# One fixed instruction order exchanged for another, found with a new account of when loads land, in an attention and gated feed-forward kernel

## The chip, the core and the metric

The kernel runs on one core of a Trainium2 chip. The metric is device time in microseconds (us) of the one launch. Five engines work side by side, each through its own instructions in the order in which they stand: TensorE (PE in the profile, with its weight loads as PEld), VectorE (DVE), ScalarE (ACT), GpSimd (POOL) and SyncE (SP), which issues every DMA of this kernel.

## What is computed

For each of 4 batches and 8 heads (768 tokens, 64 features a head) an attention over a local window and block summaries, then a gated feed-forward layer over the joined heads:

```python
k_sum = k.reshape(B, H, nb, block, D).max(axis=3)      # 24 blocks of 32 tokens
v_sum = v.reshape(B, H, nb, block, D).mean(axis=3)
mask_l = np.abs(pos[:, None] - pos[None, :]) < 16
scores = concat([where(mask_l, scale * q @ k.T, -1e9), scale * q @ k_sum.T + log(32)])
a = softmax(scores);  x = a @ concat([v, v_sum])       # (4, 768, 512)
...
xk = mu_k * x + (1 - mu_k) * x_prev;  xr = mu_r * x + (1 - mu_r) * x_prev
out = sigmoid(xr @ w_r) * (maximum(xk @ w_k, 0) ** 2 @ w_v)
```

`x_prev` is `x` one token earlier. The weights come in 64-bit floats and are unpacked on the chip.

## The kernel before

**Tiling.** Heads are taken in pairs, so a batch has four sets (`load_set`), each with the pair's keys `kt`, and its values in two halves `vx`. A set serves two units (`unit`), one for each half of the 768 tokens, each with its own query load `qt`. Unit (b, p, h) below is batch b, pair p, half h. A unit is: scores on PE (L476), mask and running minimum on DVE (L486), six exponentials on ACT (L490), the normalization on DVE, ACT or POOL (L501, L507, L512), two groups of three transposes on PE (L524), their copies (L530 on ACT, L532 on DVE), and the product with the values on PE (L539). The block maxima of the keys are taken on DVE (L412, L416, L420) and copied into `kt` on DVE or POOL (L424). In batch 0 the block means of the values come from PE (L436, then L444, with copies on ACT in L443 and L446 between and behind) and are spread into `vx` on POOL (L450). The product of a unit needs that spread.

**Feed-forward.** Mixing with the token before is L572 to L585; the gate is three products a chunk on PE (L626 to L628) and a sigmoid (L640); the first expert product is L655, its square and the split into a high and a low part L661 to L670, the second expert product L680 and L706, and the result goes out from L716. Batch b's feed-forward is interleaved with the attention of batch b+1.

**Weights.** Twenty loads of 512 KB (`weight`, L320) go through three staging tiles `st`. Each is scaled on ACT (L327), shifted and joined on DVE (L331, L335), rounded to the high part on ACT, POOL or DVE (L344, L346, L348), and the low part is a subtraction on DVE (L349).

**Order.** Nothing is scheduled at run time: the table `ORDER` lists 1910 numbered operations. A number may have a letter that sends the operation to another engine (D, A or P for DVE, ACT or POOL), and every engine gets its operations in the order in which they stand in the table. `Plan.schedule` walks the table once and gives each operation a start time from durations in `LENGTH`, hand-over times in `LATENCY` and a line of DMA figures. Those times decide three things of the program: how many filler products on a zero tile stand ahead of each real PE operation in the opening (L753, only where the plan sees PE idle), which buffer of a pool an operation gets, and which DVE operation some POOL operations have to wait for (the loop under `TIE`). All else that the DMA figures did, they did in the search that wrote the table, which is not in the file.

Of the kernel before, what the change touches and what calls it, by code (L numbers as in the profile page):

```python
# [20 lines left out]
P = 128  # L21
# [34 lines left out]
DMA_FIRST, DMA_ISSUE, DMA_START, DMA_EACH, DMA_END, DMA_BYTES_PER_NS = 740, 470, 900, 100, 1200, 400.0  # L56
FIXED_MORE = 320000
# [11 lines left out]
181 187 179 185 205 209 213 207 211 190D 1 3 4 24 191 5 193 212 43 25 6D 196 197 206 61 50 49 7 26 27 203 276 44 192D  # L69
28 45 17 92 204 214 18 210 19 194 20 52 51 80 69 208 21 215 195 216 53 46 71 217D 198 218 70 199 274 54P 219 200A 227  # L70
47 72 220 395 221 73P 234 68 300 235 372P 22 36 238 232 230 228 236 222D 252 233 231 373 396 37 237 239 229 38 253 255
39 254 62 240D 224 40 263 259 241 257 261 223 397 55 249 243D 374D 63 242D 375 64 262 264 258 256 244 225A 56 277 260
245D 376P 399 57 286 246 265D 377 58 619 324 104 585 388 65 93 81 247D 282 278 280 288 266 284 59 60 248 378D 267D 400
82 398 83 379 66 94 269 289 281 279 287 268 74 250A 301 75 270 380 98 348 643 283 285 381 290D 76 271 389 77 78 675
272 84 403 401 308 291 310 302 306 382D 292D 312 309 383 304 105 95 402 404 273 294 325 275A 313 384 390 293 295 385
86 407D 386D 589 387 99 311 307 303 296 297 405 391 408 106 85 409D 107 87 305 108 298 128 586 406 410 314D 88 411 100
89 109 394 96 393 332 315 423 101 317P 328 116 110 412 129 330 334 326 336 413 102 130 316D 97 349 90 414A 318 91 117
416 415 392 319 299A 424 118 131 119 320 421 132P 354 652 759 761 140 594 134 701 588 417D 331 41 321 422 120D 355 337
322 352 590 121 418 335 103 430 111 141 329 419 358 420 112 360 333 327 323A 425 428 142 133 113 135 338 478P 587 122
431D 647 429 474P 350 356 437 339 114 357 479 340D 341D 115 359 426A 432 427 342 361 351 353 143 433A 434 136 435 152  # L80
343 123 436 144 591 362 137 344 363 595 164 345 364 346 145 606 124 598 125 365D 438 366 439 444 599 367D 347A 153
440A 482 602 604 600 126P 644 146 596 79 368 620 369 445 480 127 154 475 370 165 155 442 371A 156 481 483 157 158 677
443 486 441 484D 476 138 607 487 147 488 451 139 605 627 477 485 489 449 452 601 446 453 603 166 167 148 490 705 149
623 150D 631 159 496 597 447A 151 608D 160 450 456 609 161 491 1145 170 577 492 646 625 629 611P 617 454A 504P 500D
501 621 448 497 578 505 614 457 168 162 163 171 493 494 579 615 172 610 648 649P 580 653 495 169 173 763 506 581 735
702 575 612 654 507 656 658 664 791 508P 502 503 455 509 498 630 499 458 510 632 459 626 463 460 461A 624 613 174D 511
464 538 175 576 665 539 659 622 462 582 471 583 465 468 512 628 584 657 704 706 660 633D 634 472 469 517 592 762 466
# [12 lines left out]
1093P 855 1056 1097 1095 926 927 1057D 1058 1121 836 838 574 1211 867 833 1036 1076 1179 930 1108 1109 856 1593 1077D  # L100
1104 1100 1105 857 858 859 1592 834 1098 1078 1106 1079 1080D 1102 1059D 860 861D 1099 1122 862 1107 868D 1060 863 931
1103 869 1081 895 932 1061 1463 1154 1094 865 1125 1062A 1101 864 1082D 1110D 1111 1127 870 1083 866 928 872 896 1594
897 898 920 921 873 874 1112D 1126 1595 922 1128 1133 871 879 875 1129 1464 1123 923 933 880 888 1131 876 877 940 1469
1124 1132 1084D 899 924 941 889D 1130 1119 1155 1085 1212 1114 1177 1113 881 1115 929 878 944 882D 1134 1135 1116 886
1158 1156 925 1166 1167 883 1468 948D 949 934 884 1086A 1159 1157 1160 1204 1117 935 1203 1210 571 887 893 885 945 890
1648 894 891A 936 892 1162 1207 1136 1137 900 937 1164 1206 1208 1209P 1479P 938 1180 1165 942 939 943 1118 1507 1138D
952D 1470 1139 1120A 1146 901 902 1187 1191 953 954D 950D 946D 1235 951 1140D 1265D 947 907 903 904 905A 1188 1163
1141 908 906 1161 955 1287D 1288 1189 912 915 956 1289D 916 1183 1181 1261 1182 1266 1185 957 1142 1262 1267D 1268
1263D 961 958 959A 1192 962 963 1190 913 1213 1184 1466 1143 1540 917 1471 975 1152 1472 1144 960 1168 1169 1531 1264
1475 1170D 1172 909 976 1186 966 964 965 1193 1171D 1173D 1218 1194 1216 910 1290 967 973 1174 1222 1223 977 978A  # L110
1175D 1214 1224 1220 968 969 1225 1195D 1238 970 1176 1647 1482 1654 971 1196D 1534 1481 911 1197 1217 1247 1248 1215
# [50 lines left out]
class Plan:  # L162
# [697 lines left out]
```

## Time and profile before

| | |
|---|---|
| median of 3 runs | 445.56 us (445.32 to 445.6) |
| the profiled execution | 445.36 us |
| its span, first to last instruction | 443.6 us |
| PE busy | 436.4 us, 98% of the span |
| DVE busy, ACT busy | 297.1 us (67%), 273.3 us (62%) |
| POOL busy | 30.9 us (7%) |
| bytes moved by DMA | 51.95 MB |

The profiled execution is 1.76 us longer than its span and 0.2 us under the median of the runs. Busy time of PE counts the fillers too, which compute nothing. The rows on which the argument rests stand in a section of their own below.

### The profile page before, as it was taken

The numbers are of one execution on the slowest core, as the hardware profiler recorded it, in microseconds if no ns is written. First come the engines' busy times: TensorE is split into PE (matmuls) and PEld (weight loads), VectorE is DVE, ScalarE is ACT, GpSimd is POOL, SyncE is SP. The second block draws the span as 40 slices with busy tenths as digits, with TensorE's granted clock in tenths as the row PEclk, the third lists the DMA queues.
The fourth block names the chain that finished last, engine by engine and source line by source line (L and its number), as shares of the span: only waits on it lengthen the run. The fifth ranks groups of instructions, "written<-read, shape, count | busy, mean of one in ns | idle before, by whom it ended". The sixth has DMA issues, their size and how long they took to land.

```text
span 443.6 us, 9603 instructions
## 1 busy us (share of the span) xinstructions
PE 436.4 (98%) x3582; PEld 375.6 (85%) x3582; DVE 297.1 (67%) x972; ACT 273.3 (62%) x807; POOL 30.9 (7%) x78
## 2 busy tenths in 40 slices
PE   7999999999999999999999999999999999999996
PEld 7877888889888888878898888888888888989885
DVE  3999989998998946648767755557643646444211
ACT  2999999885777597575466666564964315223321
POOL 0140211101030000000000210000000000000000
PEclk9999999999999999999999999999999999999999
DMA  8985868437656170141440143101200010002002
GB/s 309 401 299 194 281 249 265 149 126 227 228 141 253 55 239 27 53 153 55 134 144 19 44 117 105 51 1 42 79 1 1 2 47 1 0 1 95 0 1 95
DMA packets 26878, 51.95 MB, mean 117 GB/s; under 512 B 2512, under 2 KB 14416, under 8 KB 26832
## 3 DMA queue, kind: packets, MB, share of 16 engines
q1 hardware_dynamic: 26832, 51.35, 34.7%
q8 instruction: 28, 0.46, 0.5%
q14 instruction: 18, 0.15, 0.1%
HBM read 43.28 MB, written 6.29 MB: 112 GB/s over the span
## 4 chain that ended last, share of the span: by engine, by line
PE 87%; ACT 5%; DVE 3%; DMA 2%; issue 1%; SPq 0%; DVEq 0%; ACTq 0%
PE mm L655 28%; PE mm L680 25%; PE av L539 5%; PE pt L524 5%; PE sc L476 5%; PE mm L628 4%; PE mm L626 4%; PE mm L627 4%; PE mm L706 4%; PE av L753 2%; ACT y L490 2%; DMA st<-in_w_k 1%; DMA kt<-in_k 1%; DVE y L486 1%; ACT wc L327 1%
## 5 line engine op out<-in xcount | busy, mean ns | idle before, releaser
L655 PE MATMUL mm<-xs,wk_h 128*128 128x384 f32 x512 | 102.0, 341 | 0.6 <-DVE r L663 0.4
L655 PEld LDWEIGHTS mm<-xs,wk_h 128*128 128x128 f32 x512 | 89.5, 188 | 5.7 <-DVE r L663 1.1
L490 ACT ACTIVATE y<-y,mn 128x120 f32<-128x120 f32 x192 | 74.0, 387 | 31.0 <-DVE mn L486 30.8
L680 PE MATMUL mm<-wv_h,kh 128*128 128x512 f32 x168 | 67.2, 400 | 0.0
L680 PE MATMUL mm<-wv_l,kh 128*128 128x512 f32 x168 | 66.3, 395 | 0.0
L655 PE MATMUL mm<-xs,wk_l 128*128 128x384 f32 x256 | 55.3, 337 | 0.0
L665 ACT ACTIVATE r<-r 128x384 f32<-128x384 f32 x64 | 32.7, 520 | 35.0 <-DVE r L663 34.3
L670 DVE TENSOR_TENSOR kl<-r,kh 128x384 fp32r<-128x384 f32 x64 | 35.4, 559 | 26.7 <-ACT kh L669 18.9
L486 DVE CUSTOM_DVE_ANT_0 y<-sc,fixed_sb 128x120 f32<-128x120 f32 x192 | 47.4, 274 | 5.9 <-PE sc L476 3.7
L680 PE MATMUL mm<-wv_h,kl 128*128 128x512 f32 x168 | 49.7, 404 | 0.0
L661 ACT ACTIVATE r<-mm 128x384 f32<-128x384 f32 x42 | 20.5, 489 | 46.2 <-PE mm L655 41.6
L579 DVE SCALAR_TENSOR_TENSOR xa<-vx,fixed_sb,xa 128x384 f32<-128x384 f32 x64 | 39.1, 613 | 10.6 <-ACT xa L572 9.5
L655 PEld LDWEIGHTS mm<-xs,wk_l 128*128 128x128 f32 x256 | 45.6, 188 | 0.0
L585 DVE TENSOR_TENSOR xs<-xa,xs 128x384 fp32r<-128x384 f32 x64 | 35.1, 554 | 5.7 <-ACT xs L582 5.3
L626 PE MATMUL mm<-wr_h,xs 128*128 128x512 f32 x96 | 38.6, 402 | 0.0
L628 PE MATMUL mm<-wr_h,xs 128*128 128x512 f32 x96 | 38.0, 396 | 0.0
L627 PE MATMUL mm<-wr_l,xs 128*128 128x512 f32 x96 | 37.9, 395 | 0.0
L680 PEld LDWEIGHTS mm<-wv_h,kh 128*128 128x128 f32 x168 | 31.6, 188 | 6.2 <-DVE kh L668 0.3
L680 PEld LDWEIGHTS mm<-wv_l,kh 128*128 128x128 f32 x168 | 31.6, 188 | 6.0
L490 ACT ACTIVATION_READ_ACCUMULATOR y<-y,mn 128x1 f32 x192 | 36.3, 189 | 0.0
L680 PEld LDWEIGHTS mm<-wv_h,kl 128*128 128x128 f32 x168 | 30.2, 188 | 5.4
L524 PE MATMUL pt<-fixed_sb,y 128*120 128x128 f32 x192 | 33.2, 282 | 0.0
(76 smaller groups left out, 654.2 us busy)
## 6 DMA issues: line engine op xcount, KB each, us to landing
vx<-in_v SPq DMA_DIRECT2D x32, 384.0 KB
kt<-in_k SPq DMA_DIRECT2D x15, 544.0 KB
qt<-in_q SPq DMA_DIRECT2D x32, 192.0 KB
out<-z SPq DMA_DIRECT2D x23, 256.0 KB
st<-in_vT SPq DMA_DIRECT2D x12, 384.0 KB
st<-in_w_k SPq DMA_DIRECT2D x8, 512.0 KB
st<-in_w_v SPq DMA_DIRECT2D x8, 512.0 KB
st<-in_w_r SPq DMA_DIRECT2D x4, 512.0 KB
```

Source lines behind the costliest of these rows:

```text
L486: op("DVE", "mask", lambda h=h, i=i, var=var: nc.vector.tensor_tensor_reduce(out=y[h].t[:, i, :], in0=sc[h].t[:, i, 0:NK], in1=mask_sb[:, ...
L490: op("ACT", "exp", lambda h=h, i=i: nc.scalar.activation(y[h].t[:, i, :], y[h].t[:, i, :], AF.Exp, bias=mn[h].t[:, i:i + 1], scale=-1.0, a ...
L524: nc.tensor.transpose(out=pt.t[0:NK, i * P:(i + 1) * P], in_=y[h].t[:, i, :], identity=ident_sb)
L579: op("DVE", "mixd", lambda xt=xt, xa=xa, p=p: nc.vector.scalar_tensor_tensor(out=xa.t, in0=xt.t[:, 1 + lo:1 + lo + HT], scalar=mu_sb[:, wh ...
L585: op("DVE", "sub", lambda xa=xa, xh=xh, xl=xl: nc.vector.tensor_tensor(out=xl.t, in0=xa.t, in1=xh.t.bitcast(F32), op=ALU.subtract), reads= ...
L626: nc.tensor.matmul(ps[t].t, xh.t[:, ts], wr_h[:, p, :], start=(p == 0), stop=False)
L627: nc.tensor.matmul(ps[t].t, xh.t[:, ts], wr_l[:, p, :], start=False, stop=False)
L628: nc.tensor.matmul(ps[t].t, xl.t[:, ts], wr_h[:, p, :], start=False, stop=(p == NPAIR - 1))
L655: nc.tensor.matmul(ps.t[:, 0:HT], w[:, j, p, :], x[p][s].t, start=(n == 0), stop=(n == 11))
L665: op("ACT", "square", lambda: nc.scalar.activation(r.t, r.t, AF.Square), reads=[(r, 0)], writes=[(r, 0)])
L670: op("DVE", "sub", lambda: nc.vector.tensor_tensor(out=kl.t, in0=r.t, in1=kh.t.bitcast(F32), op=ALU.subtract), reads=[(r, 0), (kh, 0)], wr ...
L680: nc.tensor.matmul(acc[t].t, a.t[:, t * P:(t + 1) * P], w[:, j, :], start=start, stop=stop)
```

## The change

The change replaces the whole table `ORDER`, and the DMA figures with which its operations are timed. No operation is added or dropped, no duration in `LENGTH` is touched, and no tile changes its size.

```diff
-DMA_FIRST, DMA_ISSUE, DMA_START, DMA_EACH, DMA_END, DMA_BYTES_PER_NS = 740, 470, 900, 100, 1200, 400.0
-FIXED_MORE = 320000
+DMA_FIRST, DMA_ISSUE, DMA_START, DMA_EACH, DMA_END, DMA_BYTES_PER_NS, DMA_COLD = 740, 470, 1000, 50, 650, 400.0, 2240
+FIXED_MORE, KT_MORE = 0, 0
+DMA_STALL = 4200, 500
...
 ORDER = """
-29 8 9 176 0 201 2 23 32 42 12 10 11 48 67 14 13 33 34 15 16 226 35 177 30 31 188 251 178 182 180 189 183 186 184 202
+9 8 176 13 12 199 14 15 16P 29 0 2 201 23 42 10 11 48 32 67 226 177 31 30 1 180 181 184 182 251 33 183 50 49 188 178
...
-        dma, table, kind, shared = 0, None, "M", 0
+        dma, table, kind, shared = DMA_COLD, None, "M", 0
...
-                dma = max(dma, start + DMA_START) + DMA_EACH + o.size / DMA_BYTES_PER_NS
+                begin = max(dma, start + DMA_START)
+                dma = begin + DMA_EACH + o.size / DMA_BYTES_PER_NS
+                dma += DMA_STALL[1] * (begin < DMA_STALL[0] <= dma)
                 o.finish = dma + DMA_END + o.more[1]
...
-               writes=[(kt, f"k{n}")], size=P * (hi - lo) * 4, more=(0, 2 * LATE if b else 0))
+               writes=[(kt, f"k{n}")], size=P * (hi - lo) * 4 + (KT_MORE if (b, p, n) == (0, 0, 1) else 0), more=(0, 2 * LATE if b else 0))
```

Three lines are added above the code, so a line of the changed kernel has a number 3 higher than before. Three places show what the new table does; in all three `kt`, `qt`, `vx`, `st`, `wc`, `av`, `mm`, `sc` and `pt` are the tiles named above, and the number behind a name is its buffer.

SP, the first eight loads of the program, before:

```order
L386 DMA kt0_61<-in_k 128x1088
L386 DMA kt1_62<-in_k 128x528
L386 DMA kt1_62<-in_k 128x560
L465 DMA qt0_65<-in_q 128x384
L288 DMA fixed_sb_151<-in_fixed 128x556
L465 DMA qt1_66<-in_q 128x384
L320 DMA st0_136<-in_w_r 128x1024
L320 DMA st1_137<-in_w_r 128x1024
```

and now:

```order
L389 DMA kt0_61<-in_k 128x560
L389 DMA kt0_61<-in_k 128x528
L468 DMA qt0_65<-in_q 128x384
L389 DMA kt1_62<-in_k 128x1088
L291 DMA fixed_sb_151<-in_fixed 128x556
L323 DMA st0_136<-in_w_r 128x1024
L468 DMA qt1_66<-in_q 128x384
L323 DMA st1_137<-in_w_r 128x1024
```

The keys of pair 0, in two parts, and the first query load moved ahead of the keys of pair 1; the four loads ahead of `fixed_sb` (mask and constants) are the same four.

PE, from the last score of unit (0, 3, 0) over the product of unit (0, 1, 0) (`av` from `vx`), before:

```order
L476 MATMUL sc_143<-kt_64,qt_65 64x120 x2
L444 MATMUL mm_150<-sp_88,fixed_sb 24x128
L753 MATMUL av_146<-still 128x128 x7
L539 MATMUL av_146<-pts_104,vx_70 64x64
L539 MATMUL av_146<-pts_103,vx_70 64x64
...
L436 MATMUL mm_147<-vx_73,fixed_sb 32x128 x2
L436 MATMUL mm_147<-vx_72,fixed_sb 32x128 x2
...
L524 MATMUL pt_145<-fixed_sb,y_90 120x128 x3
```

and now:

```order
L479 MATMUL sc_143<-kt_64,qt_65 64x120 x2
L527 MATMUL pt_145<-fixed_sb,y_92 120x128 x3
L447 MATMUL mm_150<-sp_88,fixed_sb 24x128
L756 MATMUL av_146<-still 128x128
L439 MATMUL mm_147<-vx_74,fixed_sb 32x128 x2
L439 MATMUL mm_147<-vx_73,fixed_sb 32x128 x2
...
L756 MATMUL av_146<-still 128x128 x2
L542 MATMUL av_146<-pts_104,vx_72 64x64
L542 MATMUL av_146<-pts_103,vx_72 64x64
```

The block means of pair 2 (`mm_147`) stood behind the product and stand ahead of it, in the place of most of the fillers; the second group of transposes of unit (0, 1, 0) stood ahead of the scores of unit (0, 3, 0) and stands behind them.

POOL, the stretch that holds all of its weight roundings (L346) before:

```order
L512 TENSOR_SCALAR y_91<-y_91,rc_102 128x120 x3
L346 TENSOR_SCALAR wk_h<-wc_141 128x512
L450 COPY vx_71<-vm_84 24x768
L575 TENSOR_SCALAR xa_111<-vx_68,om_sb 128x384
L575 TENSOR_SCALAR xa_113<-vx_75,om_sb 128x384
L346 TENSOR_SCALAR wv_h<-wc_141 128x512
```

and the same part of its list now:

```order
L349 TENSOR_SCALAR wk_h<-wc_141 128x512
L349 TENSOR_SCALAR wv_h<-wc_141 128x512
L453 COPY vx_71<-vm_84 24x768
L453 COPY vx_73<-vm_85 24x768
L427 COPY kt_62<-ks_80 128x12x24
L349 TENSOR_SCALAR wv_h<-wc_141 128x512
L453 COPY vx_76<-vm_86 24x768
L349 TENSOR_SCALAR wv_h<-wc_142 128x512
L349 TENSOR_SCALAR wv_h<-wc_141 128x512
```

With two of `wr_h` further up, POOL now rounds seven weights where it rounded two; ACT rounds 10 (14 before) and DVE 3 (4 before). Over the whole program ACT has 16 of the additions of epsilon (10 before), 42 of the copies behind transposes (31) and 35 of the relu (42); DVE has the rest of each.

## Rows read from the trace of the kernel before

**Rows 1.** The page: its first line, the busy time of each engine, and the granted clock of PE in tenths, in 40 slices of the span.

```profile
span 443.6 us, 9603 instructions
PE 436.4 (98%) x3582; PEld 375.6 (85%) x3582; DVE 297.1 (67%) x972; ACT 273.3 (62%) x807; POOL 30.9 (7%) x78
...
PEclk9999999999999999999999999999999999999999
```

**Rows 2.** Busy time of each engine by stretch: the stretch and its length, then busy time and count of instructions for PE, PEld, DVE, ACT and POOL, the granted clock, the DMA share and GB/s.

```profile
0.00:10.00 10.00, 7.48 (x66) 7.13 (x67) 4.01 (x20) 2.03 (x5) 0.41 (x5) 1.00 0.82 298
...
40.00:60.00 20.00, 19.89 (x161) 16.90 (x160) 18.85 (x59) 19.13 (x50) 3.13 (x5) 1.00 0.77 263
60.00:80.00 20.00, 19.42 (x180) 16.40 (x178) 19.41 (x57) 19.89 (x61) 2.81 (x4) 1.00 0.66 221
80.00:100.00 20.00, 20.00 (x117) 16.74 (x116) 19.76 (x57) 16.53 (x45) 3.03 (x8) 1.00 0.42 136
```

**Rows 3.** The group of the fillers among the groups of instructions of PE: busy time, mean ns of one, idle time before them.

```profile
L753 PE MATMUL av<-still 128*128 128x128 f32 x112 | 16.0, 300 | 1.0 <-POOL still L747 1.0
```

**Rows 4.** The timeline of the opening: start, length, engine, line, operation, with the idle time of the engine before it and what ended it where there was any.

```profile
4.13 1.42 DVE L412 TENSOR_REDUCE kg<-kt 128x48 f32<-128x768 f32 x2 [4.13 <-DMA kt<-in_k]
6.59 0.17 DVE L416 TENSOR_REDUCE kg<-kt 128x1 f32<-128x16 f32 x1 [1.04 <-DMA kt<-in_k]
6.68 0.54 DVE L412 TENSOR_REDUCE kg<-kt 128x24 f32<-128x384 f32 x1
...
8.01 0.84 PE L476 MATMUL sc<-kt,qt 64*64 64x120 f32 x24 [1.53 <-DVE kt L424]
...
8.92 0.28 DVE L486 CUSTOM_DVE_ANT_0 y<-sc,fixed_sb 128x120 f32<-128x120 f32 x1 [0.75 <-PE sc L476]
...
9.25 0.39 ACT L490 ACTIVATE y<-y,mn 128x120 f32<-128x120 f32 x1 [7.24 <-DVE mn L486]
...
12.99 0.97 ACT L507 ACTIVATE y<-y,rc 128x120 f32<-128x120 f32 x3 [0.17 <-DVE rc L498]
...
17.69 0.94 DVE L412 TENSOR_REDUCE kg<-kt 128x48 f32<-128x768 f32 x1
17.73 0.26 ACT L446 COPY vm<-mm 24x128 f32<-24x128 f32 x1 [0.25 <-PE mm L444]
...
18.54 0.21 ACT L495 ACTIVATE sm<-sm 128x6 f32<-128x6 f32 x1
...
19.19 0.65 POOL L424 COPY kt<-ks 128x288 f32<-128x288 f32 x1
```

**Rows 5.** The timeline of SP's queue: start, length, line, what is loaded, how many in a row.

```profile
7.12 1.06 SPq L386 DMA_DIRECT2D kt<-in_k  x2
...
20.19 1.18 SPq L391 DMA_DIRECT2D vx<-in_v  x2
22.02 7.17 SPq L465 DMA_DIRECT2D qt<-in_q  x3
```

**Rows 6.** One of the sums of SP's waits: the line that waited, what it waited for, us in total, times, longest. The issue of a load waits until the load eight places ahead of it has landed.

```profile
SPq L391 <- DMA st<-in_w_r: 1.9, 2, 0.9
```

**Rows 7.** The timeline at the end of the opening, with the last large group of fillers.

```profile
24.09 1.83 PE L753 MATMUL av<-still 128*128 128x128 f32 x14
...
24.55 0.26 ACT L446 COPY vm<-mm 24x128 f32<-24x128 f32 x1
...
24.95 0.82 POOL L450 COPY vx<-vm 24x768 f32<-24x768 f32 x1 [1.20 <-DVE mn L486]
...
25.84 0.92 PE L539 MATMUL av<-pts,vx 120*64 120x64 f32 x24
...
26.69 0.86 PE L436 MATMUL mm<-vx,fixed_sb 120*32 120x128 f32 x24
```

**Rows 8.** Two of the sums of PEld's waits, at the scores and at the products with the values (line, what ended the wait, us in total, times, longest).

```profile
PEld sc L476 <- issue: 5.3, 19, 0.4
PEld av L539 <- issue: 4.1, 21, 0.4
```

**Rows 9.** The timeline of one load of `w_k` with what waited behind it on ACT, DVE and PE.

```profile
53.25 0.38 SPq L320 DMA_DIRECT2D st<-in_w_k  x1
...
58.77 0.66 ACT L327 ACTIVATE wc<-st 128x512 f32<-128x512 f32 x1 [0.81 <-DMA st<-in_w_k]
...
59.47 0.43 DVE L331 TENSOR_SCALAR wc<-wc 128x512 uint32<-128x512 uint32 x1 [0.83 <-ACT wc L327]
...
61.62 1.66 PE L655 MATMUL mm<-xs,wk_h 128*128 128x384 f32 x8 [0.45 <-DVE r L663]
```

**Rows 10.** The instructions of the line that rounds a weight on POOL: count, shortest, median and longest in ns, first and last start in us.

```profile
L346 POOL TENSOR_SCALAR wk_h<-wc x1: 992/992/992, 53.3 to 53.3; 128x512 fp32r<-128x512 f32 x1
L346 POOL TENSOR_SCALAR wv_h<-wc x1: 837/837/837, 69.5 to 69.5; 128x512 fp32r<-128x512 f32 x1
```

**Rows 11.** The same for one of the forms of the line that rounds a weight on ACT.

```profile
L344 ACT CAST wk_h<-wc x6: 604/619/627, 36.8 to 83.8; 128x512 fp32r<-128x512 f32 x6
```

**Rows 12.** The timeline of DVE around the first of the two on POOL.

```profile
52.50 1.29 DVE L335 SCALAR_TENSOR_TENSOR wc<-st,wc 128x512 uint32<-128x512 uint32 x2
...
53.28 0.99 POOL L346 TENSOR_SCALAR wk_h<-wc 128x512 fp32r<-128x512 f32 x1 [3.86 <-DVE wc L335]
...
53.91 0.95 DVE L412 TENSOR_REDUCE kg<-kt 128x48 f32<-128x768 f32 x1
```

More of the change, by code (lines that the diff above doesn't have):

```diff
@@ L73 @@
[L73 to L87, printed above, removed]
@@ new lines @@
+186 34 35 3 202 4 179 187 189 185 5 205 6P 61 24 203 276 211 209 207 204 212 210 213 190D 191 7 193D 196 208 43 206
+197 214 25 192D 26 17 44 92 27 215D 194 45 18 195 52 216 19 80 28 20 68 218 46 217 51 21 71 53 198 70 54P 227 47 72
+200A 395 219 73P 300 234 238 372P 235 236 69 36 230 237 232 22 224 228 233 220D 252 373 221 396 37 239 229 231 38 222
+259 55 240D 253 374D 39 257 274 40 261 255 260 254 241 263 56 243D 62 223 242D 262 63 264 57 375 244 258 397D 277 58
+64 245 225A 246 398 86 256 388 65P 280 93 399 324 286 284 703 81 265D 59 288 266 268 376P 701 278 247D 282 248 289
@@ new lines @@
+122 430 358 321D 350 331 360 594 425 41 329 337 643 354 103 111 588 60 428 141 420 357 123 338 142 429 426A 132D 590
+112 339 322 431D 591P 361 341 124 133 595 353 113 344 677 323A 437 340D 143 114 760 152 359 345 115 427 351 342 125
+432 355 435 433A 343 362D 606 602 126P 598 438 604 605 603 79 436 363 596 364 600 144D 620 705 153 346 647 127 145 366
+474 478 154 442 365D 367 146 134 155 347A 164 368 156 434 479 444 443 135 157 136 475 597 601 623 137 480 369 607 439
+440A 627 735 158 138P 445D 370 481 476 451 629 371A 482 441 139 486 483 147 487 484 449 477 488 452 625 450 489 485
@@ new lines @@
+1085 1155 1115 1463 1088 882 1206 1116 1166 874 1207 1162 1164 945 1158 1156 875 1086A 880 888 1212 1094 883 876 574
+1589 568 877A 1160 878 1157 1159 889 940 1132 1135D 1167 1208 1136 1138D 886 1204 571 934 884A 941 1161 890 1137 887
+893 885 935 894 891 936 1117 1119 900 937 938 1180 1118 942D 946 947 1466 939 948D 1139 902 1140D 892 1187 1209 953
+954D 1141 901 903 904 907 905A 1183 943 906 1163 908 1181 1120A 949 915 1165 950 1287 909 912 1185 955 951 1189 1592
+956 1190 1186 1265D 916 1288 961 1479 1152 957 1266 958 1191 1464 1182 1474 1188 1210 1142 1593 959 1213 962 963 1184
@@ new lines @@
+1512 1367 1551 1545 1015 1301 1514 1543 1597 1539 1311 1521D 1522 1302A 1390 1524P 1364 1590 1553 1547 1523P 1566
+1312D 1391 1504 1681 1365 1370 1018 1368D 1525 1384 1649 1303 1304 1596 1575 1573 1385 1526D 1278 1527 1282 1325 1305
+1571 1569 1386D 1306 1655 1567 1387 1309 1576 1549 1554 1310 1555 1307 1556 1374D 1308 1316 1577 1506A 1568 1326D 1369
+1570 1317 1327 1578 1328 1318 1313 1375 1314A 1574 1315 1396D 1323 1397 1528 1319 1329 1320 1621 1324 1321 1330 1332
+1599 1333D 1371 1322 1529 1656 1558 1339 1559 1606 1610 1608 1653 1572 1609 1557 1331 1530A 1340 1560 1579 1337 1607
@@ new lines @@
+1600 1604 1580 1605 1334 1602 1581P 1346 1338 1341 1342A 1335 1563 1505 1611 1601 1603 1612D 1336 1582D 1561D 1344
+1398D 1347 1376D 1348 1585 1349 1562 1343 1377 1624 1586 1679 1399 1564 1583 1727 1345 1392D 1393 1351 1613 1635 1728
+1627 1636 1633 1350 1394 1352 1584 1628 1625 1353 1395 1631 1632 1705 1400 1614 1629 1354 1372 1355 1657 1401 1373
+1587 1402 1403A 1616 1626 1615 1617D 1660 1588A 1359 1356 1405 1634 1618 1406D 1357 1407 1630 1358 1637 1619 1666 1382
+1412 1408A 1360 1658 1361 1664 1706 1665 1731 1662 1638 1639 1640D 1667 1668 1409 1659 1682 1661 1404 1620 1643 1380
@@ new lines @@
+1693 1644 1689 1413 1622 1414 1669 1663 1690 1641 1378 1381 1383 1379 1410 1707 1411 1415 1687 1683 1419 1691 1416
+1685 1670D 1729D 1732 1671 1708 1688 1684 1417 1420 1692 1421 1418 1672D 1713 1422A 1424 1730 1673 1735D 1425 1736
+1426 1423 1733D 1734 1714 1431 1427D 1715D 1428 1642D 1429 1433 1430 1432 1645 1434 1435 1674 1675D 1436 1438 1437
+1440 1439 1694 1686 1441D 1646A 1695 1696 1676 1737 1447 1442 1832 1677 1443 1444 1678 1698D 1448D 1701 1716 1449 1445
+1697D 1680A 1446 1702 1450 1739 1452 1740 1738 1451 1741 1453 1833 1709D 1457 1460 1710 1711D 1742 1699 1700D 1712
@@ new lines @@
+1717D 1718 1748 1454 1719D 1720 1455 1703 1749D 1461 1755 1743 1462 1744 1745 1806D 1750 1746A 1807 1828 1751 1721
+1752 1458 1829 1459 1722 1747 1723 1756D 1757 1753 1724 1754 1758 1725 1760 1726 1834 1808 1835 1790 1814D 1809 1759
+1761 1791 1762 1767 1763D 1764 1765A 1769 1768 1836D 1830 1766 1792 1831 1837 1815 1774 1770D 1771 1704 1775 1840D
+1776 1838D 1772 1841 1793 1794 1773 1781 1777 1839 1778 1783 1779A 1782 1784 1788 1785 1780 1818 1789 1786 1842D 1795
+1787 1796 1797 1803 1798 1800 1843 1804 1844 1805 1801 1802 1456 1849 1845D 1810D 1846 1847 1848 1863 1850D 1819 1799
@@ L143 @@
+1811 1820D 1854 1864 1865 1851 1855 1812 1852A 1853 1856 1821 1813 1861 1857D 1858 1859A 1862 1816D 1817 1868 1860
+1869 1870 1866 1867 1871 1872 1873 1875 1874 1876 1877 1882 1878D 1879 1880 1883 1881 1884 1889 1885 1886 1887A 1890
+1891 1896 1892 1893 1894 1822 1888 1895 1897 1823 1901 1898 1824 1899 1826 1825 1902 1903 1900 1904 1827 1907 1905
+1908 1906 1909
 """
```

94 lines of the change are left out of this document (35 added, 59 removed).

## The prediction

> **What bounds the kernel now.** I read the page's first lines, then the busy times by stretch, then the timeline of the opening, then the waits. PE is busy in 436.4 of 443.6 us and its clock is granted in full from the first slice to the last [rows 1], so it is the bound, and neither its products nor its clock are touched by the change. What an order can still take away is time in which PE does nothing that counts. That lies in two places. One is the opening: PE is busy only 7.48 of the first 10 us [rows 2], and 112 filler products of 16.0 us [rows 3] stand where PE would otherwise be empty; most of those 16 us are waiting in disguise. The other is the stretch from 40 to 80 us, where PE lacks 0.11 and 0.58 us, and where ACT is busy 19.89 of 20 us and DVE 19.41 [rows 2]: there the engines that feed PE are full too. From 80 to 100 us PE is full [rows 2]. So the change is worth what it shortens of the opening, plus what it does to the waits of the middle.
>
> **The opening, step by step.** In the opening PE waits for a chain of loads, DVE and ACT. Before, the first score starts at 8.01 us because the third load, a part of pair 0's keys, is first read at 6.59; the masks start at 8.92 and the first exponential at 9.25 [rows 4]. Now the two parts of those keys come first. Together they are 1088 columns, as many as the load of pair 1's keys that came first before and was read at 4.13 [rows 4]; so I take 4.13 for them. Behind that come, on DVE, the maximum of the second part (0.54), the odd columns (0.17), the joining of two maxima (under 0.2) and, now on POOL, the copy (0.65, the longer price [rows 4]), with hand-overs about 0.3: 4.13 + 0.54 + 0.17 + 0.2 + 0.65 + 0.3 = 6.0. The query load, now third, is smaller than the third load of before, so it lands between 4.13 and 6.59. The first score starts between 6.0 and 6.7 instead of 8.01.
>
> Those 1.3 to 2 us are not the gain. The masks also need `fixed_sb`, still fifth with the same four loads ahead, and DVE, which runs its list in order, has the maximum of pair 1's keys (0.94 [rows 4]) ahead of the first mask. Those keys are now the fourth load. SP issues a load when the one eight places ahead of it has landed [rows 6]; its twelfth issue, at 7.12 [rows 5], therefore dates the landing of the fourth load, and the same bytes stand up to there in both lists. 7.12 + 0.94 + about 0.1 for a small operation on `fixed_sb` gives a first mask at 8.2; the first exponential follows 0.33 behind it, as before (8.92 to 9.25 [rows 4]): 8.5. That is 0.7 earlier than before.
>
> From there ACT carries the opening. From 9.25 to 24.81, the end of the copy for the block means of pair 1 [rows 4, 7], it idles only 0.17 + 0.25 between instructions [rows 4]. I counted its list up to that copy in both orders: 18 exponentials, three scalings, three copies behind transposes, two roundings, two normalizations, four copies of block means, one evacuation, one mix in each, and one addition of epsilon (0.21 [rows 4]) that now stands on DVE. So the copy ends at 8.5 + 15.56 - 0.21 = 23.9 if the idle time stays, 23.4 if it goes; I take 23.7. Behind it POOL's spread and the hand-overs took 25.84 - 24.81 = 1.03 [rows 7], which gives the product of unit (0, 1, 0) at 24.7 instead of 25.84: 1.1 earlier. And the block means of pair 2, 26.69 to 27.5 behind that product before [rows 7], now stand ahead of it in the place of fillers, which is another 0.8 us of real work that is already done. The loads allow it. Up to the second value load of pair 1, place 16, the lists hold the same sixteen loads, and the issue at 20.19 [rows 5] dates its landing. The next two value loads moved ahead of one weight load; the issue at 22.02 [rows 5] dates the landing at place 18 before, and one more load behind it lands about 1 us later (the step from 20.19 to 22.02 is two loads): 23. Those means then end at 23.9, ahead of 24.7. **The opening is worth 1.1 + 0.8 = 1.9 us**; if the block means of pair 1 or a DVE step come late by 0.5 it is 1.4, if ACT never idles 2.2.
>
> **Changes of kind on PE.** Each time PE goes over to scores or to a product with values from other work, its weight load stands still for a moment: 5.3 us in 19 places at the scores, 0.28 each, and 4.1 in 21 at the products, 0.20 each [rows 8]. Counted in the two orders, scores are entered from transposes or large products 21 times instead of 26, products with values and block means 19 times instead of 15; the others follow each other directly. That is -5 x 0.28 + 4 x 0.20 = -0.6. Three more times PE goes from transposes to a large product, which has no row of its own; its price lies between 0 and 0.28. So the term lies between -0.6 and 0.2; I take **-0.3**, in the middle of what is left if the new exits cost 0.1 each.
>
> **The middle.** Five more weights are rounded on POOL: 0.84 to 0.99 each there [rows 10] against 0.62 on ACT [rows 11]. What waits is the subtraction on DVE behind it, and with it everything queued on DVE, which is full (19.41 and 19.76 of 20 us [rows 2]). Two of the new five have little DVE work between rounding and subtraction in the list; I charge them 0.3 each on DVE and a third of that on PE: **+0.2**, between 0 (other work on DVE covers it, and ACT is relieved of four roundings) and 1. Loads of weights can still come late. The one case of before is issued at 53.25 and read at 58.77; ACT stood 0.81 for it, DVE 0.83 behind that, and PE 0.45 [rows 9]. The new list still has loads of queries, values and keys ahead of weights in the same stretch, so I leave this loss as it is: 0, between -0.6 (gone) and +1.2 (twice more).
>
> The tail, from the last second product to the last store, has the same operations in the same order, so it costs the same.
>
> **Sum.** 445.36 - 1.9 - 0.3 + 0.2 = 443.4 us for a profiled execution; that of before lies 0.2 us under the median of the runs, so **443.6 us** for the median.
>
> **Rivals.** *The gain is given back.* From 40 to 80 us ACT and DVE are full [rows 2]; a PE that comes 2 us earlier asks for their results 2 us earlier. ACT's chain itself starts only 0.7 us earlier. If ACT and DVE and not PE set the pace there, what remains is those 0.7, and one more late load like that of rows 9 (0.45 to 0.6 on PE) takes the most of it: 445.56 - 0.7 + 0.5 = 445.4, between 444.7 and 446.2. Against it: PE lacks only 0.7 us in those 40 us [rows 2], so PE is still the nearer bound, and four roundings leave ACT.
>
> *POOL holds DVE.* While POOL rounds the weight at 53.28, DVE is still in its second L335, which ends on time (two in 1.29), and the POOL instruction is the long one of the two, 0.99 against 0.84; DVE's L412 behind it takes 0.95 as elsewhere 0.94 [rows 4, 10, 12]. So in that row POOL waited and DVE did not. It need not fall so: if POOL comes first and DVE stands through each of the five, with a DVE that is 97% full the loss goes on to PE: 5 x 0.92 = 4.6 us, 443.6 + 4.6 = 448.2. It ends slower than before from about 2.9 us on, that is from three of the five in full. The Trainium skill has this as a rule (SBUF — State Buffer, "Who interferes with whom"): an instruction of VectorE with two inputs in SBUF and one of GpSimd that reads SBUF exclude each other, and the one that starts first blocks the other for its whole length. By that rule, the trace agrees as far as the row at 53.28 goes, where DVE came first; no row shows the other order.
>
> *More than forecast.* The late load disappears and the two roundings are covered: 443.6 - 0.6 - 0.2 - 0.3 = 442.5, down to 441.9.
>
> *The change does not do what it says*, since the new figures describe the loads no better: then the first score stays near 8 us and the opening gives 0.8 at most, which is within the first rival's time.
>
> **Chances.** A difference of 0.2%, 0.9 us, is about what a measurement of this kernel can tell from no change. The forecast, 442.6 to 444.6, has 0.70; given back, 0.17; POOL holds DVE, 0.06; more than forecast, 0.07. The range of 442.4 to 445.2 holds the forecast, half of the first rival and a little of the last, 0.8 in all. Faster by over 0.2% (under 444.67): 0.70 + 0.07 = 0.77; within 0.2%: 0.17; slower by over 0.2%: 0.06.
>
> **What would show it.** First score at 6.0 to 6.7 us, first exponential at 8.5, the copy of pair 1's block means ending near 23.7, the product of unit (0, 1, 0) near 24.7 with the means of pair 2 ahead of it: each right or wrong by itself. In the middle: PE's busy time from 40 to 80 us no more than 0.7 us short, POOL's roundings 0.84 to 1 us long, L349 and L335 on DVE no longer than before. The forecast is wrong if the first exponential is not earlier than 9.0, or if the product of unit (0, 1, 0) is 1 us earlier and the end is not: then the middle took it, and the waits of ACT for `st` and of DVE for POOL say which way.

## The result: slower by 0.68%

| | before | after |
|---|---|---|
| median of 5 runs (lowest to highest), us | 445.40 (445.11 to 445.60) | 448.29 (447.24 to 449.00) |
| profiled execution, us | 445.36 | 448.97 |
| its span, us | 443.6 | 447.2 |

After to before is 1.0068, with a 95% interval of 1.0057 to 1.0080. The forecast was 443.6 us, and the time lies outside its range. The runs of after also lie further apart, 1.8 us against 0.5.

The page of after: its first line, the busy times and the granted clock, then the shares of the chain that ended last by engine.

```profile
span 447.2 us, 9584 instructions
PE 437.1 (98%) x3570; PEld 374.2 (84%) x3570; DVE 291.6 (65%) x958; ACT 273.7 (61%) x818; POOL 34.6 (8%) x85
...
PEclk9999999999999999999999999999999999999999
...
PE 79%; ACT 11%; DMA 6%; DVE 2%; issue 1%; SPq 0%; DVEq 0%; ACTq 0%
```

The clock is full in both [rows 1]. The same line of the chain before:

```profile
PE 87%; ACT 5%; DVE 3%; DMA 2%; issue 1%; SPq 0%; DVEq 0%; ACTq 0%
```

So ACT and DMA held 7% of it and now hold 17%. The busy times by stretch (columns as in [rows 2]) and the fillers say where:

```profile
0.00:10.00 10.00, 7.90 (x69) 7.58 (x70) 3.48 (x18) 2.15 (x6) 0.86 (x7) 1.00 0.81 286
...
40.00:60.00 20.00, 19.57 (x158) 16.48 (x156) 18.09 (x60) 18.49 (x49) 4.40 (x5) 1.00 0.74 255
60.00:80.00 20.00, 19.01 (x175) 16.21 (x176) 19.13 (x60) 19.12 (x59) 2.48 (x4) 1.00 0.52 174
80.00:100.00 20.00, 17.76 (x100) 13.44 (x99) 16.87 (x45) 15.36 (x35) 1.45 (x4) 1.00 0.64 212
```

```profile
L756 PE MATMUL av<-still 128*128 128x128 f32 x100 | 15.1, 307 | 1.0 <-POOL vx L550 1.0
```

The opening is better: the fillers fell from 112 to 100 [rows 3]. (PE's busy time in the first 10 us, 7.90 against 7.48 [rows 2], does not decide it: over all traces here it is 7.5 to 8.7 with the old opening and 7.7 to 9.0 with the new one.) From 40 to 100 us, where PE lacked 0.69 us of 60 before [rows 2], it now lacks 0.43 + 0.99 + 2.24 = 3.66.

**A ledger.** Since the two orders do different work at one moment, I also counted PE's lag: the time, less the PE work done by then, where each operation of PE counts as much as the kernel's own table of figures gives it. Those figures serve as weights only; all work adds up to 408.2 us in every kernel here, so the lags of two orders can be subtracted. Fillers and waits both show as lag. From one profiled run each, in us:

| at | before | after | urgent_only | urgent_first | st4 | urgent_first_st4 |
|---|---|---|---|---|---|---|
| 25 | 17.8 | 17.0 | 17.8 | 17.0 | 17.0 | 17.0 |
| 55 | 21.2 | 19.8 | 21.2 | 20.0 | 19.8 | 20.0 |
| 80 | 23.1 | 22.6 | 22.8 | 21.9 | 22.8 | 20.9 |
| 100 | 23.5 | 26.4 | 25.9 | 22.8 | 24.2 | 21.5 |
| 120 | 24.1 | 27.4 | 26.8 | 24.3 | 25.1 | 22.5 |
| end | 35.4 | 39.0 | 38.1 | 35.8 | 36.6 | 34.0 |

(The other columns belong to runs below. The trace of urgent_only is of an execution of 448.12 us, 1.8 above the median of that run, and its opening is late by itself (last section), so its column stands for a slow execution.) After is 1.4 us ahead of before at 55 us. From 55 to 80 it loses 0.9, from 80 to 100 another 3.4, later 0.7: 3.6 at the end, the difference of the spans. So after was ahead when the opening ended, and the middle took that and more.

**The opening of after**, from its timeline:

```profile
3.47 1.19 DVE L415 TENSOR_REDUCE kg<-kt 128x24 f32<-128x384 f32 x2 [3.47 <-DMA kt<-in_k]
...
5.01 0.42 POOL L427 COPY kt<-ks 128x288 f32<-128x288 f32 x1 [4.05 <-DVE ks L423]
...
6.63 0.85 PE L479 MATMUL sc<-kt,qt 64*64 64x120 f32 x24 [1.12 <-DMA qt<-in_q]
...
7.88 0.95 DVE L415 TENSOR_REDUCE kg<-kt 128x48 f32<-128x768 f32 x1 [2.93 <-DMA kt<-in_k]
...
9.14 0.40 ACT L493 ACTIVATE y<-y,mn 128x120 f32<-128x120 f32 x1 [7.13 <-DVE mn L489]
...
23.81 0.86 PE L439 MATMUL mm<-vx,fixed_sb 120*32 120x128 f32 x24
...
25.24 0.92 PE L542 MATMUL av<-pts,vx 120*64 120x64 f32 x24
```

The keys are read at 3.47 and the copy for the first score starts at 5.01, but the score waits for the query until 6.63, and DVE stands 2.93 us for the fourth load, until 7.88. The first exponential comes at 9.14, 0.11 earlier than before, which is within what the traces differ by: 8.70 to 9.42 in the nine with the new opening, 8.88 to 9.25 in the five with the old one. The product of unit (0, 1, 0) starts at 25.24, 0.6 earlier than in [rows 7], and the block means of pair 2 (23.81) now stand ahead of it.

**The middle of after.** The first place, at 58 us, on SP's queue, ACT, DVE, POOL and PE in turn:

```profile
51.31 3.20 SPq L323 DMA_DIRECT2D st<-in_w_v  x2
...
58.04 1.24 ACT L330 ACTIVATE wc<-st 128x512 f32<-128x512 f32 x2 [1.33 <-DMA st<-in_w_v]
...
59.31 0.43 DVE L334 TENSOR_SCALAR wc<-wc 128x512 uint32<-128x512 uint32 x1 [1.74 <-ACT wc L330]
...
60.38 0.42 POOL L427 COPY kt<-ks 128x288 f32<-128x288 f32 x1 [3.45 <-DVE ks L423]
...
60.85 0.85 PE L479 MATMUL sc<-kt,qt 64*64 64x120 f32 x24 [1.15 <-POOL kt L427]
```

And the second, around wv7, the last piece of `w_v`:

```profile
80.58 0.33 SPq L370 DMA_DIRECT2D st<-in_vT  x1
...
85.25 0.68 DVE L338 SCALAR_TENSOR_TENSOR wc<-st,wc 128x512 uint32<-128x512 uint32 x1
...
86.00 0.33 SPq L323 DMA_DIRECT2D st<-in_w_v  x1
...
92.06 0.66 ACT L330 ACTIVATE wc<-st 128x512 f32<-128x512 f32 x1 [3.25 <-DMA st<-in_w_v]
...
92.75 0.43 DVE L334 TENSOR_SCALAR wc<-wc 128x512 uint32<-128x512 uint32 x1 [3.06 <-ACT wc L330]
...
93.14 0.54 PE L527 MATMUL pt<-fixed_sb,y 128*120 128x128 f32 x3 [1.41 <-ACT pts L533]
...
94.56 0.50 PE L683 MATMUL mm<-wv_l,kh 128*128 128x512 f32 x1 [0.65 <-DVE wv_l L352]
```

It is the pattern of [rows 9] (load, ACT, DVE, PE) at larger size: ACT runs its list in order, so the scaling of a piece that has not landed holds all that is queued on ACT, then DVE, then PE. The name that PE waits for (POOL's copy, ACT's `pts`) is only the last link. The sum of ACT's waits for pieces of `w_v`, and the three pieces of the chain that ended last (start, length):

```profile
ACT wc L330 <- DMA st<-in_w_v: 5.4, 3, 3.3
```

```profile
51.31 6.71 DMA st<-in_w_v
...
65.38 6.25 DMA st<-in_w_v
...
86.00 5.98 DMA st<-in_w_v
```

Before, ACT's only wait for a piece of a weight was 0.81 us [rows 9].

Why they come late can be counted. For each piece I took from the trace when its load was issued, when its last part reported and when ACT began to scale it (us; the time to spare is from that report to the scaling):

| piece | issued, landed, read, after | spare, after | spare, before | spare, urgent_first_st4 |
|---|---|---|---|---|
| wv0 | 27.8, 31.6, 42.3 | 10.7 | 1.3 | 10.9 |
| wv2 | 51.3, 58.0, 58.0 | 0.0 | 4.6 | 2.7 |
| wv4 | 65.4, 71.6, 71.7 | 0.0 | 0.5 | 2.6 |
| wv5 | 63.7, 69.5, 76.9 | 7.4 | 1.3 | 10.1 |
| wk7 | 70.1, 73.5, 82.0 | 8.5 | 0.3 | 9.2 |
| wv7 | 86.0, 92.0, 92.1 | 0.1 | 1.9 | 11.1 |

There are three staging tiles, and a piece holds one from its issue until DVE has combined it. In after some pieces lie there landed for 7 to 11 us (before: 4.6 at most), and others get a tile too late. wv7 is issued at 86.00, when DVE has combined wk7 (the row at 85.25); wk7 had held that tile since 70.1. The tile that came free before that went to the load of block means' values at 80.58.

### The profile page after: what moved, and what is told of

It reads as the page before. It is cut to its first block, busy times and chain, and to the rows that moved or that the text cites. A ratio compares the mean times of both kernels' runs of the same rounds, so it can differ in the third digit from the quotient of the medians.

```text
span 447.2 us, 9584 instructions
## 1 busy us (share of the span) xinstructions
PE 437.1 (98%) x3570; PEld 374.2 (84%) x3570; DVE 291.6 (65%) x958; ACT 273.7 (61%) x818; POOL 34.6 (8%) x85
## 4 chain that ended last, share of the span: by engine, by line
PE 79%; ACT 11%; DMA 6%; DVE 2%; issue 1%; SPq 0%; DVEq 0%; ACTq 0%
PE mm L658 27%; PE mm L683 23%; PE pt L527 4%; PE av L542 4%; DMA st<-in_w_v 4%; PE mm L629 4%; PE mm L630 4%; PE mm L631 4%; PE sc L479 4%; PE mm L709 4%; ACT y L493 3%; ACT wc L330 2%; DMA kt<-in_k 1%; ACT y L510 1%; PE av L756 1%
## 5 line engine op out<-in xcount | busy, mean ns | idle before, releaser
L489 DVE CUSTOM_DVE_ANT_0 y<-sc,fixed_sb 128x120 f32<-128x120 f32 x192 | 46.5, 274 | 16.2 <-PE pt L527 14.0
L668 ACT ACTIVATE r<-r 128x384 f32<-128x384 f32 x64 | 33.0, 522 | 37.2 <-DVE r L666 36.6
L664 ACT ACTIVATE r<-mm 128x384 f32<-128x384 f32 x35 | 17.1, 489 | 49.6 <-PE mm L658 47.1
L588 DVE TENSOR_TENSOR xs<-xa,xs 128x384 fp32r<-128x384 f32 x64 | 34.9, 552 | 9.1 <-ACT xs L585 8.3
L683 PEld LDWEIGHTS mm<-wv_l,kh 128*128 128x128 f32 x168 | 31.6, 188 | 7.1 <-DVE wv_l L352 1.3
L683 PEld LDWEIGHTS mm<-wv_h,kh 128*128 128x128 f32 x168 | 31.6, 188 | 6.7 <-DVE kh L671 0.7
```

The source lines that it names most:

```text
L489: op("DVE", "mask", lambda h=h, i=i, var=var: nc.vector.tensor_tensor_reduce(out=y[h].t[:, i, :], in0=sc[h].t[:, i, 0:NK], in1=mask_sb[:, ...
L588: op("DVE", "sub", lambda xa=xa, xh=xh, xl=xl: nc.vector.tensor_tensor(out=xl.t, in0=xa.t, in1=xh.t.bitcast(F32), op=ALU.subtract), reads= ...
L668: op("ACT", "square", lambda: nc.scalar.activation(r.t, r.t, AF.Square), reads=[(r, 0)], writes=[(r, 0)])
L683: nc.tensor.matmul(acc[t].t, a.t[:, t * P:(t + 1) * P], w[:, j, :], start=start, stop=stop)
```

## The experiments

**Theory T1**: the new table gives the weights' pieces too little lead, in tiles and in places on SP's list; that costs more than the opening gains. **Rivals**: the new figures do it by themselves; POOL's roundings hold DVE; the opening's gain is given back because ACT and DVE set the pace anyway. Each run has 6 to 12 times beside 23 to 35 of the kernel before; the ratio is to the kernel before. In kernels with an edited table a line number is one lower than in after (L329 is L330).

**figures_only.** After, with before's table.

```
-ORDER = """ 9 8 176 13 12 199 14 15 16P 29 0 2 201 ...
+ORDER = """ 29 8 9 176 0 201 2 23 32 42 12 10 11 ...
```

> The changed code with all its new figures for loads, but with the table ORDER of the kernel before. It tells the table from what the figures do by themselves (tile slots, order of the scheduled loads, filler products). Theory T1 (the table gives weight loads too little lead): as before, 445.4 +- 0.4. Rival 'the figures themselves': near 448.3. Rival 'POOL's roundings hold DVE': as before, since none of the table's new POOL roundings is in it.

Measured: 445.19 us, ratio 1.0007 (0.9998 to 1.0015). The figures cost nothing; the table does. Its lag at the end is 35.0 against 35.4, and at 55 us 20.8 against 21.2, so lags of one order differ by 0.4 from run to run.

**head_new and head_old.** The two tables, cut behind operation 223, the product of unit (0, 1, 0); what a prefix already holds is left out behind it.

```
 head_new: after's table up to 223, then before's order
 head_old: before's table up to 223, then after's order
```

> The new table up to the product of unit (0,1,0), the end of the opening, and from there the instructions in the order of the kernel before. T1: the opening keeps its 1.4 us and the weight loads have their old lead, so 443.5 to 444.6, faster than both. Rival 'the opening's gain is given back later, since ACT and DVE set the pace': 445.2 to 445.6.

> The reverse: the old table up to the product of unit (0,1,0), the new order behind it. T1: the loss of the middle without the gain of the opening, 449 to 450.2. Rival 'the gain of the opening is given back': the opening is worth nothing, so 448.3 or less.

Measured: head_new 445.06 us, 1.0006 (0.9990 to 1.0022); head_old 448.73, 1.0088 (1.0070 to 1.0106). The loss sits behind the opening, as T1 says; head_old is 0.20% above after, which would make the opening worth 0.9 us, within the intervals, and its time lies between T1's 449 and the rival's 448.3. But the new opening ahead of the old order brings nothing, where T1 wanted 1.4 us: a miss. Its profiled run was one of three (of 12) near 447 us, and there the second value load of pair 0 landed at 16.5 us (14.9 in after), and a load of keys behind it was late too:

```profile
17.85 0.17 DVE L418 TENSOR_REDUCE kg<-kt 128x1 f32<-128x16 f32 x1 [1.16 <-DMA kt<-in_k]
```

**wv7_first.** One exchange on SP's list.

```
-SP load means1 (577)
+SP load wv7 (170)
...
-SP load wv7 (170)
-DVE vred means1 (578)
+SP load means1 (577)
...
+DVE vred means1 (578)
```

> The new table with one pair of loads exchanged: the weight piece wv7 is issued ahead of the third load of block means' values instead of behind it (the reader of the values' load moves back by 22 places). T1: ACT's 3.25 us of waiting for wv7 at 92 us goes, and PE's 1.67 + 0.99 us behind it, so 445.4 to 446.4. Rival 'POOL or DVE holds PE there': no change, 448.3 +- 0.5.

Measured: 447.41 us, 1.0052 (1.0038 to 1.0065). The wait for wv7 is gone (spare time 5.0 us), but the time is 1 us above what T1 gave. PE's gaps behind that wait are the 1.41 and 0.65 us of the rows above, not the 1.67 and 0.99 of the expectation. Part of it is a new wait: the exchanged load now comes late for DVE.

```profile
99.54 0.95 DVE L371 TENSOR_REDUCE vs<-st 128x24 f32<-128x768 f32 x1 [1.17 <-DMA st<-in_vT]
```

**urgent_only and urgent_first.** Five loads that are read 30 us later or more go behind the pieces that are read next; the second also has the exchange.

```
 SP load wv1 (98)
-SP load unit110 (652)
-SP load set12 (702)
-SP load set22 (1145)
 SP load wk5 (140)
...
 SP load set11 (643)
-SP load unit111 (677)
-SP load set13 (760)
+SP load unit110 (652)
+SP load set12 (702)
+SP load set22 (1145)
 SP load wk6 (152)
...
 SP load wv4 (134)
+SP load unit111 (677)
+SP load set13 (760)
```

> The changed kernel with five loads on SP's list that are read 30 us later or more (queries of units 110 and 111, values of sets 12 and 13, keys of set 22) moved behind the weight pieces and the query of unit 100 that are read within 8 us; nothing on another engine moves. T1: the waits for wk5, wv2 and wv4 at 58 and 71 us go and the one for wv7 at 92 us stays: ratio 1.001 to 1.005. Rival 'POOL or DVE holds PE': 1.0057 to 1.008.

> The five loads moved back and wv7 exchanged with the load of block means' values as in the run before. T1: the gain of the opening (1.1 to 1.4 us) shows with little of the loss: ratio 0.997 to 1.003. Rival: the exchange alone gave 1.0052, so if the middle's other waits don't come from these loads, 1.004 to 1.0065.

Measured: urgent_only 446.34 us, 1.0026 (1.0011 to 1.0041); urgent_first 445.39, 1.0002 (0.9988 to 1.0016). Moving six loads and one reader takes the whole loss away. The two edits add up within the intervals: 0.42% and 0.16% of the 0.68% alone, 0.66% together. The ledger's 3.4 us from 80 to 100 of one run of after is thus more than wv7 costs on the median. Some loss is left in the trace of urgent_first: ACT still waits 1.2 us for a piece of `w_v`, and from 80 to 120 us the lag grows by 2.4 us, before's by 1.0.

**st4.** A fourth staging tile, the same table.

```
-        st=tiles("st", 3, [P, 1024], U32), wc=tiles("wc", 4, [P, 512], U32),
+        st=tiles("st", 4, [P, 1024], U32), wc=tiles("wc", 4, [P, 512], U32),
```

> The changed kernel with four staging tiles for the pieces of the weights instead of three, and nothing else: the same table, but each piece is issued a tile earlier (its load no longer waits for the piece three places ahead). T1 (the new table gives the weights' loads too little lead): most of the loss goes, ratio to before 0.997 to 1.002 (444 to 446). Rival 'POOL's roundings hold DVE' or 'ACT and DVE are simply full': ratio as the changed kernel's, 1.0057 to 1.008.

Measured: 445.96 us, 1.0015 (1.0003 to 1.0028), as T1 said. No instruction of an engine changed its place, so POOL's roundings and the loads of ACT and DVE are as in after; what changed is when pieces are issued.

**no_pool_cast.** The five roundings behind the opening that came to POOL go back to ACT and DVE; two of the seven stay on POOL.

```
-65P 108P 102P 138P 150P
+65  108  102  138  150D
```

> The changed kernel with its five roundings on POOL behind the opening put where the kernel before had them (four on ACT, one on DVE). Rival 'POOL's roundings hold DVE': faster than the changed kernel, ratio under 1.004. T1: POOL is not in the way and ACT, which is full there, gets 0.6 us a piece more, so no gain: ratio 1.006 to 1.011.

Measured: 448.92 us, 1.0084 (1.0056 to 1.0112). The rival on POOL falls: without these five the kernel is no faster.

**before_st4 and wv7_late.** Two controls on the kernel before: the fourth tile alone, and the late piece alone.

```
 before_st4:
-        st=tiles("st", 3, ...
+        st=tiles("st", 4, ...
 wv7_late:
 SP load set22 (1145)
-SP load wv7 (170)
 SP load means1 (577)
 SP load means1 (579)
+SP load wv7 (170)
```

> The kernel before with four staging tiles instead of three, nothing else. If the fourth tile helps the new table because that gives the loads too little lead (T1), it does little here, where ACT hardly waits for a load: ratio 0.998 to 1.001. If more staging helps any order, the fourth tile's gain in the new table (0.5%) says nothing of the table: ratio 0.995 to 0.997.

> The kernel before with its weight piece wv7 issued behind two loads of block means' values instead of ahead of them (it then starts some 3 us later), nothing else. T1: the old order loses as the new one does at that place, ratio 1.002 to 1.006 (0.9 to 2.7 us). Rival 'a load 3 us later is hidden by other work, the new order's loss lies elsewhere': 0.999 to 1.0015.

Measured: before_st4 444.25 us, 0.9985 (0.9974 to 0.9996); wv7_late 445.58, 1.0012 (0.9999 to 1.0024). The fourth tile helps the old order a little, 0.15%, against 0.53% in the new one. wv7_late is a miss of T1: its 1.0012 lies in the rival's range, and no loss is certain. ACT did stand for the late piece,

```profile
85.95 0.69 ACT L326 ACTIVATE wc<-st 128x512 f32<-128x512 f32 x1 [1.50 <-DMA st<-in_w_v]
```

but ACT is busy only 16.53 of 20 us there in the old order [rows 2], and its waits for PE's products from 76 to 100 us fell from 3.2 to 1.9 us. So in the old order most of this wait, if not all, was made up elsewhere, and the lateness of a load alone does not tell its cost.

**head_new_st4 and urgent_first_st4.** The cut order, and the new order with both edits of SP's list, with four tiles.

```
 head_new_st4     = head_new     + tiles("st", 4, ...)
 urgent_first_st4 = urgent_first + tiles("st", 4, ...)
```

> The new table up to the product of unit (0,1,0), the order of the kernel before behind it, and four staging tiles. The ledger of PE's time of the run with three tiles has the opening's gain lost in the same stretch in which one load came 2 us late. If it is lost to loads that come late in the opening: ratio 0.996 to 0.999. If ACT and DVE take it back: 0.9995 to 1.002.

> The new table with both edits of SP's list (the five loads that are read late moved back, wv7 ahead of the load of block means' values) and four staging tiles: every weight piece has the most lead. T1: the best of the new order, ratio 0.996 to 0.9995. If the loss that is left (1.0002 with three tiles) does not come from the weights' loads: 0.9995 to 1.002.

Measured: head_new_st4 444.51 us, 0.9985 (0.9973 to 0.9997); urgent_first_st4 443.96, 0.9973 (0.9961 to 0.9985), the lowest median here and faster than both kernels. In it no piece of `w_k` or `w_v` has under 1.9 us to spare, and PE is full from 60 to 100 us:

```profile
40.00:60.00 20.00, 19.84 (x171) 16.94 (x173) 19.79 (x66) 19.94 (x55) 4.82 (x6) 1.00 0.75 248
60.00:80.00 20.00, 20.00 (x183) 17.21 (x173) 19.87 (x60) 19.94 (x60) 2.68 (x4) 1.00 0.71 244
80.00:100.00 20.00, 20.00 (x118) 16.69 (x118) 19.55 (x54) 17.45 (x48) 0.83 (x3) 1.00 0.58 196
```

But before_st4 is as full there (19.98 and 20.00 of 20 us), and with the fourth tile in both the new order is only 0.3 us ahead: 443.96 against 444.25 us, ratios of 0.9973 and 0.9985 whose intervals overlap. So with the late loads gone, little of the forecast's 2.0 us is left at the end.

head_new_st4 met its number for the wrong reason: before_st4 has the same ratio without the new opening. Their ledgers part and meet again: at 25 us the new opening is 0.8 ahead (17.0 against 17.8), at 30 us 0.3, at 120 us 0.3. In those 5 us, head_new_st4 and before_st4 in turn:

```profile
25.00:30.00 5.00, 4.88 (x68) 3.75 (x68) 4.53 (x12) 4.87 (x16) 1.46 (x4) 1.00 0.95 333
```

```profile
25.00:30.00 5.00, 5.00 (x89) 3.90 (x89) 5.00 (x22) 4.92 (x18) 1.67 (x4) 1.00 0.84 298
```

ACT is full in both, so it is likely that in the old order ACT's list takes the gain back at once, which is the third rival; that is argued from these rows, no run tried it. In the new order the gain lasts to 55 us.

## Why the prediction was wrong

**The step that failed** is the term for late loads of weights, put at 0 with bounds of -0.6 and +1.2. Its mechanism was right, and it was named with [rows 9]; its size was off. Moving six loads and one reader gives back 0.66%, 2.9 us, and with a fourth tile 0.95%, 4.2 us, of which 0.15% came to the old order too. So the term was about +3, most of the 4.7 us between the forecast and the time. The rest lies in the opening and the changes of kind, both below, and in what is given back behind the opening; it is not separated further. The reason given for 0 was that both lists hold other loads ahead of weights in the same stretch. That compares the lists and not the lead: how long before its reader each piece is issued, which hangs on which tile comes free when. Both can be read from the order before any run: which pieces are loaded early and scaled late (wv0, wv5, wk7), and what stands ahead of the next piece on SP's list.

**The opening**, 1.9 us, was mis-sized. In this pair of traces it is 1.4 (25.84 to 25.24 is 0.6, and the means of pair 2 that now stand ahead are 0.8 to 0.9), the lower end of its bounds, and the ledger agrees at 55 us. But the trace of before has the latest opening of its kind: that product starts at 25.5 to 25.8 in the five traces with the old opening, at 25.1 to 25.5 in seven of the nine with the new one, and at 26.4 and 26.5 in the two where a load of values was late. The lag at 55 us is 20.8 to 21.2 in the four traces of the old order and 19.8 to 20.0 in the five of the new order that have POOL's roundings and no such late load. So the opening is worth about 0.9, under its lower bound. The first score at 6.63 was within 6.0 to 6.7. The first exponential at 9.14 was not the 8.5 forecast, and by the prediction's own sign (not earlier than 9.0) the forecast failed there already: the step "the same bytes stand up to there" dated the fourth load at 7.12, and it was read at 7.88. ACT's list then ran as counted: the copy of pair 1's means, forecast to end at 23.7, ended at 24.2.

**Changes of kind**, -0.3, did not come. The sums of PEld's waits rose [rows 8]; this is after:

```profile
PEld sc L479 <- issue: 6.2, 19, 1.3
...
PEld av L542 <- issue: 5.0, 23, 0.4
```

The count of entries in the order (21 scores instead of 26) does not show here: 19 waits as before. What this is worth on PE is not separated; behind 120 us, where no weight is loaded any more, the ledger has after 0.3 us longer.

**POOL's roundings**, +0.2, were nearer 0 or below: after to no_pool_cast is 0.16% in their favour, within the intervals. The four of one form took 0.62 us each and not 0.84 to 1:

```profile
L349 POOL TENSOR_SCALAR wv_h<-wc x4: 617/618/619, 54.2 to 80.6; 128x512 fp32r<-128x512 f32 x4
...
46.91 0.84 POOL L349 TENSOR_SCALAR wk_h<-wc 128x512 fp32r<-128x512 f32 x1 [5.50 <-DVE wc L338]
```

```profile
46.74 0.53 DVE L504 TENSOR_TENSOR y<-y,rc 128x360 f32<-128x360 f32 x1
```

The one of 0.84 began while DVE was in an operation with two inputs (`y` and `rc`); DVE's took 0.53, as the one at 45.70 did, and POOL's was the longer. The trace of after has the other order too, with a mix on POOL and then with a rounding:

```profile
29.83 0.59 POOL L578 TENSOR_SCALAR xa<-vx,om_sb 128x384 f32<-128x384 f32 x1
...
30.02 0.77 DVE L504 TENSOR_TENSOR y<-y,rc 128x360 f32<-128x360 f32 x1
...
74.26 0.62 POOL L349 TENSOR_SCALAR wv_h<-wc 128x512 fp32r<-128x512 f32 x1 [7.39 <-DVE wc L338]
...
74.69 0.59 DVE L588 TENSOR_TENSOR xs<-xa,xs 128x384 fp32r<-128x384 f32 x1
```

Here POOL came first and DVE paid: 0.77 instead of 0.53 for L504, 0.59 instead of 0.55 for L588. By the rule of the Trainium skill (SBUF — State Buffer, "Who interferes with whom") the one that starts first blocks the other. The trace agrees in both orders. The prediction's "no row shows the other order" holds for the rows that it shows, not for the trace of before:

```profile
70.45 0.82 POOL L450 COPY vx<-vm 24x768 f32<-24x768 f32 x1
...
71.06 0.76 DVE L349 TENSOR_TENSOR wv_l<-wc,wv_h 128x512 fp32r<-128x512 f32 x1
```

(The subtraction took 0.76 there; its median is 0.69.) So POOL can hold DVE, but the rival's price did not come: of after's seven roundings only the one at 74.26 came ahead of such an operation of DVE, and it cost 0.04 us, not the 0.92 that the rival charged for each.

**The rivals and chances.** "The gain is given back" ended at 446.2 at most because it allowed one more late load at 0.45 to 0.6; the chain that ended last has three. It had the right place and the wrong price, so the chance of slower, 0.06, was drawn from the POOL case alone, which was the wrong one. "The change does not do what it says" did not hold as it was put: the first score did come earlier. But the new figures are short for weights: a 512 KB load with nothing ahead comes to 1000 + 50 + 650 ns and 1310 ns for its bytes, 3.0 us, where before's figures gave 3.5. Measured from issue to the last report, the pieces of `w_k` and `w_v` took 3.2 to 8.4 us in after, median 5.0, and 3.2 to 8.1, median 4.4, in before. Whether a search with longer times would have kept the lead was not tried.

## What to carry to other kernels

When an order of work is moved, list for each load its issue, its landing and its reader, before the engines are weighed: on an engine that runs in order, one piece with no time to spare holds everything queued behind it, and the engine that shows the wait is two or three links away. Staging tiles are part of the order: pieces that land early and are read late take the lead from the others. A gain at the start must be followed to a place where the bound engine stays full; here a ledger of the bound engine's work by time showed in one table where it was kept and where it went.

## What was not expected of the hardware

In the opening of after the 192 KB query load, issued at 1.63, was read at 6.63, and the fourth load was read 0.76 us later than the dating from before's list gave, though as many bytes stood ahead of it. The other traces bear it out: the fourth load landed at 6.8 to 7.1 us in the five with the old opening and at 7.4 to 8.1 in the nine with the new one. So the order in which loads of different size are issued, and not only their bytes, moved when the next ones landed; why is not shown.

A load of 512 KB is landed when the last of its sixteen parts reports, and one part can be late alone: for wv7 in after fifteen reports came from 89.0 to 90.5 and the last at 92.0, where before's came within 0.3 us. The two traces whose times lie 1.7 and 1.8 us above the median of their runs, head_new and urgent_only, are those in which the second value load of pair 0 landed at 16.5 and 16.6 us, against 13.8 to 15.2 in the other twelve; in both, fifteen parts had reported by 14.7. The same kernel's runs lay 1.8 us apart in after, 3.6 in st4 and 1.9 in urgent_first_st4, against 0.5 for before in the first comparison (2.4 to 3.4 in the later ones, with 23 to 35 runs); that single slow loads make this spread is likely from the two traces, not shown for the rest.
